# Transposing K and Q through a DRAM scratch by DMA instead of on TensorE, in an attention plus gMLP kernel

## The chip, the cores and the metric

The kernel runs on one core of one Trainium2 chip. The metric is device time in microseconds (us) of one execution; lower is better. Each comparison below was made with runs of the kernel before on the same chip in the same rounds, and "faster" or "slower" needs a difference of 2%. An interval in brackets is a 95% interval.

Engines are called by the profile's names: PE is TensorE, PEld its weight load, DVE VectorE, ACT ScalarE, POOL GpSimd, SP SyncE, which issues most DMAs here. "SPq" is SP's queue of DMA issues. "L326" is line 326 of the kernel's file. A line of the changed kernel has another number than the same line of the kernel before: the K and Q evacuation is L512 before and L523 after, the general matmul helper L326 and L328, the residual add L874 and L885.

## The reference, cut to what matters

```python
# q, k, v: (4 batches, 8 heads, 768, 64); blocks of 32; x: (4, 768, 512)
scores = (q @ k.transpose(0, 1, 3, 2)) / sqrt(64)
# kept: window |bi - bj| <= 1, first and last block row and column, 3 random key blocks per query block
attn = softmax(where(mask, scores, -1e9)) @ v
x = attn.transpose(0, 2, 1, 3).reshape(4, 768, 512)
h = gelu(x @ w_in); u, vv = h[..., :512], h[..., 512:]
vv = layernorm(vv) * g_ln
vv = einsum('ts,bsd->btd', w_sg, vv) + b_sg
return x + (u * vv) @ w_out
```

The scores need K and Q with the head dimension on the partitions, and they arrive with tokens on the partitions. So both have to be transposed, for each batch.

## The kernel before

A small list scheduler inside the kernel (`Plan`) is given every operation with a modelled duration, simulates the engines, and so fixes the order of instructions on each engine. On the chip every engine works through its list in that order and waits by semaphores. If something lands later than the model thought, whatever stands behind it on that engine waits too. The model of a DMA is one shared pipe:

```python
if o.dsem is not None:                     # a DMA
    b = max(free[e] + 0.9, dmafree)
    dmafree = b + o.bytes                  # nbytes / 390e3 us, or the op's own bw
    o.fin = dmafree + 1.1
```

An argument `aft=` orders operations in this plan only; it makes no semaphore. One use of it matters: the exponentials of a batch are planned after the last U gelu of the batch before, to save ACT table loads.

The parts that the change and the argument touch (cuts marked):

```python
def loads(b):                              # batches 1 to 3: POOL queue, f32 -> bf16 on the way
    ...
    for nm, t_, src in (("v", vn, v), ("k", kn, k), ("q", qn, q)):
        o = op("POOL", f"ld{nm}{b}", ..., w=[(nm + "n", n) for n in range(4)],
               nbytes=1572864, bw=265e3, aft=aft)

def transposes(b):
    for pp in range(4):
        for nm, n_ in (("k", kn), ("q", qn)):
            u = Unit("M")                  # one of two PSUM slots, shared with the MLP
            ...                            # 12 PE transposes into the slot
            op("PE", f"TR{nm}{b}.{pp}", tr, ...)
            # DVE empties the slot for K, ACT for Q, into KT / QT
            op("ACT" if nm == "q" else "DVE", f"e{nm}{b}.{pp}", ev, ...)
    op("DVE", f"eq{b}.d", ...)             # QT columns 768:800 <- 0:32
    op("DVE", f"ek{b}.g", kg, r=KT...)     # KG <- the first and last key block of KT
# kgather: the random key blocks, KR <- KT, copied by DVE (L596) and POOL (L600)
# weights2: w_sg and w_out loaded, planned after batch 1's loads of v, k and q
for b in range(4):
    ... attention of batch b; after its second tile loads(b + 1), vprep(b + 1) ...
    transposes(b + 1); vread(b + 1)
    if b == 0: weights2(hold["kq"], hold["kq"])
    ... MLP of batch b: V, U, spatial gate S (with w_sg), O (with w_out), residual add ...
```

I call the stretch from one batch's last exponential to the next batch's first one a handover. The MLP's V and U parts of the batch before, and most of the transposes, run in it.

The softmax here doesn't subtract the row's maximum and nothing guards it: scores larger than these inputs give would overflow.

Of the kernel before, what the change touches and what calls it, by code (L numbers as in the profile page):

```python
# [7 lines left out]
BF16 = mybir.dt.bfloat16  # L8
# [4 lines left out]
B, H, S, D = 4, 8, 768, 64  # L13
P, T = 128, 6
DM, DFF = 512, 1024
NB = 24
EPS = 1e-6
NRING = 16
NKR = 8
ORDERS = ((0, 1, 2, 3, 4, 5), (5, 0, 1, 2, 3, 4))  # L20
SPSET = (3, 6, 9, 12, 15, 18, 21)
# [18 lines left out]
class Plan:  # L40
# [10 lines left out]
    def op(self, eng, name, fn, r=(), w=(), dur=0.1, lat=0.0, prio=0, mode=None, alloc=None, use=None, dsem=None, nbytes=0, pre=(), nd=1, aft=(), bw=390e3):  # L51
        o = Op()
        o.eng, o.name, o.fn, o.dur, o.lat, o.prio, o.mode = eng, name, fn, dur, lat, prio, mode
        o.alloc, o.unit, o.dsem, o.bytes = alloc, use, dsem, nbytes / bw
        o.nd = nd
        o.start = o.fin = None
        o.idx = len(self.ops)
        deps = {}
        for k in r:
            x = self.lastw.get(k)  # L60
            if x is not None:
                deps[x.idx] = x
        for k in w:
            x = self.lastw.get(k)
            if x is not None:
                deps[x.idx] = x
            for x in self.readers.get(k, ()):
                deps[x.idx] = x
        if use is not None:
            use.readers.append(o)  # L70
        if dsem is not None:
            x = self.dlast.get(dsem)
            if x is not None:
                deps[x.idx] = x
            self.dlast[dsem] = o
        for k in w:
            self.lastw[k] = o
            self.readers[k] = []
        for k in r:
            self.readers.setdefault(k, []).append(o)  # L80
        o.deps = list(deps.values())
        aft = {x.idx: x for x in aft}
        for k in pre:
            for x in self.readers.get(k, ()):
                aft[x.idx] = x
        o.after = [x for x in aft.values() if x.idx not in deps]
        self.ops.append(o)
        return o
# [164 lines left out]
def bass_bigbird_attn__then__gmlp_full_block_kernel(  # L253
# [6 lines left out]
    op = pl.op  # L260

    def sb(name, shape, dt):
        return ctx.enter_context(nc.sbuf_tensor(name, shape, dt))
# [16 lines left out]
    qn = sb("qn", [P, H, T, D], BF16)  # L280
    kn = sb("kn", [P, H, T, D], BF16)
    vn = sb("vn", [P, H, T, D], BF16)
    vj = sb("vj", [P, T, H, 65], BF16)
    QT = sb("QT", [P, 4, 800], BF16)
    KT = sb("KT", [P, 4, 800], BF16)
    KG = sb("KG", [P, 4, P], BF16)
# [3 lines left out]
    VG = sb("VG", [P, 4, 130], BF16)  # L290
    VR = sb("VR", [P, NRING, H, 65], BF16)
    PW = [sb(f"PW{i}", [P, 1024], BF16) for i in range(4)]
    PR = [sb(f"PR{i}", [P, 1024], BF16) for i in range(3)]
    PG = [sb(f"PG{i}", [P, 512], BF16) for i in range(3)]
    rden = [sb(f"rden{i}", [P, 2, 4, 1], F32) for i in range(2)]
    lnst = sb("lnst", [P, 4, 6], F32)
    lnmv = sb("lnmv", [P, T, 2], F32)
# [14 lines left out]
    Mps = ctx.enter_context(nc.psum_tensor("Mps", [P, 1024], F32))  # L312
    Mbf = Mps.bitcast(BF16)
    scr = [nc.dram_tensor(f"scr{i}", (800, 520), BF16, kind="Internal").ap() for i in range(2)]
    pl.pool("S", 2)
    pl.pool("O", 1)
    pl.pool("M", 2)
# [47 lines left out]
    def c_bias1(vx):  # L365
# [8 lines left out]
       r=["VGz"] + [("VG", n) for n in range(4)], w=[("scz", 0)], dur=0.6, prio=-60, dsem="z0", nbytes=33000)  # L374

    op("SP", "sbi", lambda e: e.dma_start(sbi[:, :], sampled_blocks.bitcast(I32)), w=["sbi"], dur=0.6, prio=-300,
       dsem="c0", nbytes=600)
# [18 lines left out]
    def ixr(x):  # L396
# [7 lines left out]
       r=["effr", "ident"], w=["ixp"], dur=0.1, prio=-170, alloc=u_ix)  # L404
# [86 lines left out]

    def transposes(b):
        pr = 1000 * b - 350 if b else -70
        for pp in range(4):
            for nm, n_ in (("k", kn), ("q", qn)):
                u = Unit("M")
                TT = KT if nm == "k" else QT

                def tr(pe, pp=pp, n_=n_, u=u):
                    ins = None  # L500
                    for j in range(T):
                        c = u.slot * 1024 + j * P
                        for hp in range(2):
                            ins = pe.transpose(Mbf[64 * hp:64 * hp + 64, c:c + P], n_[:, 2 * pp + hp, j, :], ident[:, :])  # L504
                    return ins
                tk = [(nm.upper() + "T", pp)]
                op("PE", f"TR{nm}{b}.{pp}", tr, r=[(nm + "n", pp), "ident"], w=[("trp", nm, b, pp)], dur=0.36, prio=pr + pp, mode="64c", alloc=u, pre=tk)

                def ev(x, pp=pp, nm=nm, u=u, TT=TT):
                    o_ = TT[:, pp, 0:S].rearrange("p (t j) -> p t j", j=T)  # L510
                    i_ = Mbf[:, u.slot * 1024:u.slot * 1024 + S].rearrange("p (j t) -> p t j", t=P)
                    return x.activation(o_, i_, ACT.Copy) if nm == "q" else x.tensor_copy(o_, i_)  # L512
                op("ACT" if nm == "q" else "DVE", f"e{nm}{b}.{pp}", ev, r=[("trp", nm, b, pp)], w=tk, dur=0.86, prio=pr + pp, use=u)
        op("DVE", f"eq{b}.d", lambda x: x.tensor_copy(QT[:, :, 768:800], QT[:, :, 0:32]), r=[("QT", p_) for p_ in range(4)], w=[("QT", 4)], dur=0.15, prio=pr + 4)

        def kg(x):
            ins = None
            for hp in range(2):
                for i, c0 in enumerate((0, 736)):
                    ins = x.tensor_copy(KG[64 * hp:64 * hp + 64, :, 64 * hp + 32 * i:64 * hp + 32 * i + 32], KT[64 * hp:64 * hp + 64, :, c0:c0 + 32])  # L520
            return ins
        op("DVE", f"ek{b}.g", kg, r=[("KT", p_) for p_ in range(4)], w=["KG"], dur=0.5, prio=pr + 4)
# [30 lines left out]
    rgof, krof = {}, {}  # L553
    cnt = {"PW": 0, "PR": 0, "PG": 0, "gt": 0, "rd": 0, "KR": 0, "VR": 0}

    def ring(nm, n):
        x = cnt[nm] % n
        cnt[nm] += 1
        return x
# [4 lines left out]
    def vgather(n):  # L564
# [3 lines left out]
        if b == 0:  # L568
            pr = -20 + tau
        rg = n % NRING  # L570
        rgof[b, i] = rg
# [57 lines left out]
    def attention(b, tau, pos):  # L629
        bp = b % 2  # L630
        pr = 1000 * b + 100 * pos
# [5 lines left out]
        krs = [krof[b, i0 + ib] for ib in range(nbk)]  # L637
        qk = [("QT", t) for t in range(5)]
        kt = [("KT", t) for t in range(4)]
        pw, pg_, pr_ = ring("PW", 4), ring("PG", 3), ring("PR", 3)  # L640
        ga = hold.get("g", []) if b else []

        uW = Unit("S")
# [1 line left out]
        def qkw(pe):  # L645
            ins = None
            for pp in range(4):
                for g_ in range(ng):
                    for hp in range(2):
# [3 lines left out]
                        ins = mm(pe, Sps[:, c:c + 64], KT[r0:r0 + 64, pp, kc:kc + P],  # L653
                                 QT[r0:r0 + 64, pp, 32 + P * tau + 64 * g_:96 + P * tau + 64 * g_], True)
            return ins
        op("PE", f"qkW{b}.{tau}", qkw, r=qk + kt, w=[("sW", b, tau)],
           dur=0.015 * 8 * ng + 0.1, prio=pr, mode="64x128", alloc=uW, pre=[("PW", pw, 0), ("PW", pw, 1)])
# [15 lines left out]
        def qkg(pe):  # L673
            ins = None
            for pp in range(4):
                c = uG.slot * 1024 + pp * P
                ins = mm(pe, Sps[:, c:c + P], KG[:, pp, :], QT[:, pp, 32 + P * tau:160 + P * tau], True)
            return ins
        op("PE", f"qkG{b}.{tau}", qkg, r=qk + ["KG"], w=[("sG", b, tau)], dur=0.22, prio=pr + 1, mode="128", alloc=uG, pre=[("PG", pg_)])
        op("ACT", f"exG{b}.{tau}", aft=ga, fn=lambda a: a.activation(PG[pg_][:, :], Sps[:, uG.slot * 1024:uG.slot * 1024 + 512], ACT.Exp, scale=SCALE),  # L680
           r=[("sG", b, tau)], w=[("PG", pg_)], dur=0.6, prio=pr + 1, mode="exp", use=uG)

        uR = Unit("S")

        def qkr(pe):
            ins = None
            for pp in range(4):
                for ib in range(nbk):
                    for hp in range(2):
                        r0 = 64 * hp  # L690
                        c = sbank(uR, hp) + (pp * nbk + ib) * 32
                        qc = 32 * (i0 + ib)
                        ins = mm(pe, Sps[:, c:c + 32], KR[r0:r0 + 64, pp, krs[ib], :], QT[r0:r0 + 64, pp, qc:qc + 32], True)
            return ins
        op("PE", f"qkR{b}.{tau}", qkr, r=qk + [("KR", rg, j) for rg in krs for j in range(3)], w=[("sR", b, tau)],
           dur=0.013 * 8 * nbk + 0.1, prio=pr + 2, mode="64x128", alloc=uR, pre=[("PR", pr_)])
# [8 lines left out]
        if last:  # L705
            for c3 in range(3):
# [3 lines left out]
                def qkq(pe, c3=c3, uQ=uQ):  # L710
# [12 lines left out]
                   r=[("sQ", b, c3)], w=[("PW", pw3, 0), ("PW", pw3, 1)], dur=1.02, prio=pr + 3 + c3, mode="exp", use=uQ)  # L723
# [16 lines left out]
        def pvw(pe):  # L740
# [9 lines left out]
           w=[("Oa", b, tau)], dur=0.014 * 8 * ng + 0.05, prio=pr + 51, mode="64")  # L750

        def pvr(pe):
# [8 lines left out]
           dur=0.009 * 8 * nbk + 0.05, prio=pr + 52, mode="32")  # L761
        ow = [("Oa", b, tau), ("Ob", b, tau)]
        for c3, pw3 in enumerate(pq):
            def pvq(pe, c3=c3, pw3=pw3):
# [8 lines left out]
               w=[("Oq", b, c3)], dur=0.45, prio=pr + 53, mode="64")  # L773
# [3 lines left out]
           r=ow, w=[("rd", rd)], dur=0.13, prio=pr - 500, use=uO)  # L777
# [84 lines left out]
    def mlp_o(b, tau):  # L862
# [21 lines left out]

    loads(0)  # L885
    transposes(0)
    vprep(0)
    vread(0)
    op("POOL", "w_in", lambda g: g.dma_start(w_in[:, :, :], moe_w_in.rearrange("(a p) f -> p a f", p=P)), w=["w_in"], dur=1.2,
       prio=WP, dsem="w0", aft=[hold["sc"]], nbytes=2.1e6)  # L890
    ng = used = 0
    for b in range(B):
        for pos, tau in enumerate(ORDERS[b > 0]):
            while ng < len(gseq) and ng < used + NRING and gseq[ng][0] == b:
                vgather(ng)
                ng += 1
            if pos == 2 and b + 1 < B:
                loads(b + 1)
                vprep(b + 1)
            while ng < len(gseq) and ng < used + NRING and (gseq[ng][0] == b or pos > 2):  # L900
                vgather(ng)
# [5 lines left out]
        if b + 1 < B:  # L907
            transposes(b + 1)
            vread(b + 1)
            while ng < len(gseq) and ng < used + NRING:  # L910
                vgather(ng)
# [46 lines left out]
```

## Time and profile before

The recorded time before is 282.72 us (2 runs, 282.61 to 282.83). The prediction was made from a trace whose own execution took 316.53 us, with a span of 314.7 us. These are lines of that first page: the span, and the chain of work that ended last, by engine.

```profile
span 314.7 us, 8868 instructions
...
PE 58%; DVE 14%; issue 11%; ACT 9%; POOL 3%; another core or an unknown queue 2%; DVEq 1%; POOLq 0%; ACTq 0%
```

PE is the engine that most of the chain runs through, but 11% of the chain is "issue", time in which the engine waited for nothing that the profile shows. The table of busy time by stretches (columns: stretch; for each engine busy us and instructions; PE clock granted; DMA share; GB/s) gave the handovers of this trace (the first one is shown) and a dense stretch for comparison:

```profile
80.80:97.00 16.20, 7.94 (x145) 6.20 (x142) 6.99 (x27) 4.44 (x7) 8.88 (x12) 0.82 1.18 232
...
248.00:280.00 32.00, 29.87 (x736) 21.97 (x735) 20.73 (x60) 20.98 (x32) 7.49 (x18) 1.00 0.17 49
```

PE was busy about half of this handover stretch and nearly all of the dense one. That is the slack the change aims at.

For comparing with the kernel after I use a later trace of the same kernel from the 282 us chip (run b_third). Its page says:

```profile
span 282.4 us, 8868 instructions
PE 220.7 (78%) x3717; PEld 162.8 (58%) x3717; DVE 163.5 (58%) x468; ACT 149.1 (53%) x222; POOL 103.8 (37%) x204
DMA packets 34411, 41.29 MB, mean 146 GB/s; under 512 B 6548, under 2 KB 27700, under 8 KB 34372
PE 61%; DVE 16%; ACT 10%; DMA 5%; issue 3%; SPq 2%; POOL 1%; DVEq 0%; POOLq 0%; ACTq 0%
```

Here is its handover to batch 1 in the chain of work that ended last (columns: start us, us, what):

```profile
80.28 0.80 PE Mps L504 x11
81.10 0.82 ACT QT L512
...
88.88 0.87 PE Sps L326 x12
...
93.26 0.49 ACT uT L841
...
95.06 0.84 ACT PW L668 x2
```

Twelve transposes on PE (L504), an evacuation on ACT (L512), twelve more, and so on; then the last MLP matmuls, the last U gelu (L841) and the first exponential of batch 1 (L668) at 95.06 us. This alternation is what the change removes.

### The profile page before, as it was taken

The numbers are of one execution on the slowest core, as the hardware profiler recorded it, in microseconds if no ns is written. First come the engines' busy times: TensorE is split into PE (matmuls) and PEld (weight loads), VectorE is DVE, ScalarE is ACT, GpSimd is POOL, SyncE is SP. The second block draws the span as 40 slices with busy tenths as digits, with TensorE's granted clock in tenths as the row PEclk, the third lists the DMA queues.
The fourth block names the chain that finished last, engine by engine and source line by source line (L and its number), as shares of the span: only waits on it lengthen the run. The fifth ranks groups of instructions, "written<-read, shape, count | busy, mean of one in ns | idle before, by whom it ended". The sixth has DMA issues, their size and how long they took to land.

```text
span 314.7 us, 8868 instructions
## 1 busy us (share of the span) xinstructions
PE 234.8 (75%) x3717; PEld 171.5 (55%) x3717; DVE 163.7 (52%) x468; ACT 149.1 (47%) x222; POOL 104.8 (33%) x204
## 2 busy tenths in 40 slices
PE   1543047597737479787699999787799997999994
PEld 1432036485626357565355868565567675767642
DVE  6525013236533165425498657354477665758683
ACT  2587024356334752636212587455425874755200
POOL 1131777112183851542441222653403124102100
PEclk9999999969795758779799999899599999999999
DMA  6957863980999929331799102442711014111022
GB/s 205 374 164 288 230 162 78 173 133 40 195 275 242 308 33 214 86 92 38 206 210 261 64 6 50 133 122 60 211 68 32 4 27 120 37 69 35 0 100 100
DMA packets 34411, 41.29 MB, mean 131 GB/s; under 512 B 6548, under 2 KB 27700, under 8 KB 34372
## 3 DMA queue, kind: packets, MB, share of 16 engines
q0 software_dynamic: 14112, 17.40, 27.9%
q1 hardware_dynamic: 20260, 23.33, 24.0%
q8 instruction: 29, 0.48, 0.6%
q14 instruction: 10, 0.08, 0.1%
HBM read 39.45 MB, written 9.55 MB: 156 GB/s over the span
## 4 chain that ended last, share of the span: by engine, by line
PE 58%; DVE 14%; issue 11%; ACT 9%; POOL 3%; another core or an unknown queue 2%; DVEq 1%; POOLq 0%; ACTq 0%
PE Mps L326 28%; PE Ops L326 12%; PE Sps L326 9%; PE Mps L795 5%; PE Mps L504 4%; DVE gt L856 3%; ACT PR L700 2%; DVE xg L859 2%; DVE KT L512 2%; ACT QT L512 2%; POOL VR L579 1%; PE Mps L620 1%; DVE x_tok L780 1%; DVE x_tok L874 1%
## 5 line engine op out<-in xcount | busy, mean ns | idle before, releaser
L579 POOL DMA_INDIRECT VR<-scr,IDX x60 | 56.2, 937 | 56.7 <-PE Ops L326 29.7
L596 DVE COPY KR<-KT 128x128 bf16 x176 | 27.4, 230 | 38.7 <-PE Ops L326 20.8
L326 PE MATMUL Mps<-w_sgT,vh 128*128 128x384 bf16 x192 | 38.0, 345 | 2.7 <-DVE KT L512 1.8
L700 ACT ACTIVATE PR<-Sps 96x1024 bf16<-96x1024 f32 x20 | 20.4, 1020 | 32.9 <-PE Ops L326 21.6
L600 POOL COPY KR<-KT 128x128 bf16 x88 | 22.5, 296 | 39.1 <-PE Sps L326 27.1
L326 PE MATMUL Mps<-w_out,xg 128*128 128x512 f32 x96 | 28.6, 429 | 2.8 <-DVE xg L859 1.6
L326 PE MATMUL Mps<-xg,w_in 128*128 128x384 f32 x128 | 28.3, 375 | 2.5 <-ACT QT L512 2.0
L856 DVE SCALAR_TENSOR_TENSOR gt<-Mps,gcol,bsg 128x384 f32<-128x384 f32 x32 | 19.8, 618 | 17.8 <-PE Mps L326 15.6
L326 PE MATMUL Mps<-w_in,xg 128*128 128x512 f32 x96 | 27.6, 434 | 1.5 <-ACT xg L798 0.7
L326 PE MATMUL Sps<-QT,KR 64*128 64x32 bf16 x704 | 13.6, 178 | 19.2 <-POOL KR L600 9.7
L798 ACT ACTIVATE xg<-Mps 128x512 fp32r<-128x512 f32 x24 | 14.3, 596 | 28.3 <-PE Mps L795 21.0
L326 PEld LDWEIGHTS Mps<-xg,w_in 128*128 128x128 f32 x128 | 23.3, 205 | 6.9 <-ACT QT L512 2.3
L326 PEld LDWEIGHTS Mps<-w_sgT,vh 128*128 128x128 bf16 x192 | 17.6, 101 | 16.9 <-DVE KT L512 2.2
L814 ACT ACTIVATE vg<-Mps 128x512 f32<-128x512 f32 x24 | 14.0, 598 | 26.8 <-PE Mps L326 25.2
L326 PE MATMUL Sps<-QT,KT 64*128 64x64 bf16 x544 | 16.9, 209 | 12.7 <-issue 3.8
L821 POOL TENSOR_TENSOR lnt<-lnmv,lnc 128x2 f32<-128x2 f32 x12 | 3.0, 248 | 69.7 <-DVE lnmv L817 69.7
L512 DVE COPY KT<-Mps 128x768 bf16<-128x768 bf16 x16 | 15.1, 954 | 20.3 <-PE Mps L504 17.2
L326 PE MATMUL Ops<-VA,PW 128*64 128x65 bf16 x384 | 21.7, 206 | 3.9 <-issue 3.7
L326 PEld LDWEIGHTS Sps<-QT,KR 64*128 64x128 bf16 x704 | 10.9, 96 | 23.3 <-POOL KR L600 9.8
L326 PEld LDWEIGHTS Mps<-w_in,xg 128*128 128x128 f32 x96 | 18.0, 204 | 8.6 <-DVE x_tok L874 2.0
L326 PEld LDWEIGHTS Mps<-w_out,xg 128*128 128x128 f32 x96 | 16.9, 193 | 9.6 <-DVE xg L859 2.5
L326 PEld LDWEIGHTS Sps<-QT,KT 64*128 64x128 bf16 x544 | 12.1, 105 | 17.9 <-issue 5.5
(91 smaller groups left out, 414.0 us busy)
## 6 DMA issues: line engine op xcount, KB each, us to landing
out_dram<-x_tok SPq DMA_DIRECT2D x20, 256.0 KB, 2.1
scr<-vj SPq DMA_DIRECT2D x4, 780.0 KB, 5.0
VR<-scr SPq DMA_DIRECT2D x84, 32.5 KB, 3.3
VS<-scr SPq DMA_DIRECT2D x4, 650.0 KB
vn<-in_v_dram POOLq DMA_DIRECT2D x3, 768.0 KB, 9.1
kn<-in_k_dram POOLq DMA_DIRECT2D x3, 768.0 KB
qn<-in_q_dram POOLq DMA_DIRECT2D x3, 768.0 KB, 13.9
VA<-scr SPq DMA_DIRECT2D x4, 520.0 KB
```

Of the source, the lines that this page charges most:

```text
L326: return pe.matmul(o, l, r, start=start, stop=True, skip_group_check=True)
L504: ins = pe.transpose(Mbf[64 * hp:64 * hp + 64, c:c + P], n_[:, 2 * pp + hp, j, :], ident[:, :])
L512: return x.activation(o_, i_, ACT.Copy) if nm == "q" else x.tensor_copy(o_, i_)
L579: return g.indirect_dma_start(out=VR[0:96, rg, :, :].rearrange("p h e -> p (h e)"), out_offset=None, in_=scr[bp][:, :], in_offset=bass.Ind ...
L596: ins = x.tensor_copy(KR[:, :, rg, 32 * j:32 * j + 32], KT[:, :, bass.ds(vals["DVE", j, i], 32)])
L600: op("POOL", f"kp{b}.{i}", lambda x, i=i, rg=rg: x.tensor_copy(KR[:, :, rg, 64:96], KT[:, :, bass.ds(vals["POOL", 2, i], 32)]), r=kk + [(" ...
L700: return a.activation(PR[pr_][0:96, :], Sps[0:96, uR.slot * 1024:uR.slot * 1024 + 1024], ACT.Exp, scale=SCALE)
L795: ins = pe.transpose(Mps[:, cc:cc + P], x_tok[bp][:, tau, kt * P:kt * P + P], ident_f[:, :])
L798: op("ACT", f"xE{b}.{tau}", lambda a: a.activation(xg[c][:, :, tc * P:tc * P + P], Mps[:, u.slot * 512:u.slot * 512 + 512].rearrange("p (a ...
L814: op("ACT", f"gV{b}.{tau}", lambda a: a.activation(vg[vr][:, :], Mps[:, u.slot * 512:u.slot * 512 + 512], ACT.Gelu_apprx_tanh), r=[("vp", ...
L856: op("DVE", f"g1{b}.{c}{dt}", lambda x: x.scalar_tensor_tensor(gt[gr][:, :], Mps[:, u.slot * 512:u.slot * 512 + 384], gcol[:, dt:dt + 1], ...
L859: op("DVE", f"g2{b}.{c}{dt}", lambda x: x.tensor_tensor(xg[2 + c][:, dt, :], gt[gr][:, :], uT[c][:, dt, :], ALU.mult), r=[("gt", gr), ("uT ...
```

## The change

The intent is to free PE, the shared PSUM slots, DVE and ACT of the transposes of batches 1 to 3. DVE permutes K and Q once to token rows of 512 contiguous values, SP writes them to DRAM, and a transposing DMA brings each back as KT or QT. The space for the permuted copy `kj` comes from two rings (16 to 14 and 3 to 2 buffers). The diff, with its headers and one line that repeats a ring's size left out:

```diff
-NRING = 16
+NRING = 14
+    kj = sb("kj", [P, T, H, D], BF16)
-    PG = [sb(f"PG{i}", [P, 512], BF16) for i in range(3)]
+    PG = [sb(f"PG{i}", [P, 512], BF16) for i in range(2)]
+    skq = {nm: nc.dram_tensor(f"scr_{nm}", (768, 512), BF16, kind="Internal").ap() for nm in "kq"}
     def transposes(b):
         pr = 1000 * b - 350 if b else -70
-        for pp in range(4):
+        if b:
+            for nm, n_, TT in (("k", kn, KT), ("q", qn, QT)):
+                op("DVE", f"p{nm}{b}", lambda x, n_=n_: x.tensor_copy(kj[:, :, :, :], n_[:, :, :, :].rearrange("p h j d -> p j h d")),
+                   r=[(nm + "n", n) for n in range(4)], w=["kj"], dur=0.9, prio=pr - 300)
+                op("SP", f"w{nm}{b}", lambda e, nm=nm: e.dma_start(skq[nm].rearrange("(p j) c -> p (j c)", j=T), kj[:, :, :, :].rearrange("p j h d -> p (j h d)")),
+                   r=["kj"], w=[("skq", nm)], dur=0.6, prio=pr - 300, dsem=f"w{nm}", nbytes=786432)
+            for nm, TT in (("k", KT), ("q", QT)):
+                op("SP", f"T{nm}{b}", lambda e, nm=nm, TT=TT: e.dma_start_transpose(TT[:, :, 0:S], skq[nm]),
+                   r=[("skq", nm)], w=[(nm.upper() + "T", p_) for p_ in range(4)], dur=0.6, prio=pr, dsem="xbar", nbytes=786432)
+        for pp in range(4 if b == 0 else 0):
             for nm, n_ in (("k", kn), ("q", qn)):
```

There is one `kj` for K and Q, both reads share the semaphore `xbar`, so K is read before Q, and writes and reads all go through the in-order SP queue.

More of the change, by code (lines that the diff above doesn't have):

```diff
@@ L639, in attention @@
         kt = [("KT", t) for t in range(4)]
-        pw, pg_, pr_ = ring("PW", 4), ring("PG", 3), ring("PR", 3)
+        pw, pg_, pr_ = ring("PW", 4), ring("PG", 2), ring("PR", 3)
         ga = hold.get("g", []) if b else []
```

## The prediction

> **What bounds the kernel now.** One core, 282.7 us timed; the profiled execution spans 314.7 us, so I scale by 0.90. PE is busy 75% of the span and holds 58% of the chain that ended last (busy section, chain). Away from handovers PE is nearly full (table of busy time by stretches: 17.5 of 18 us in 227 to 245, 29.9 of 32 in 248 to 280). It is loose where one batch hands over to the next: 7.9 of 16.2 us in 80.8 to 97.0, 9.4 of 14.4 in 142.8 to 157.2, 9.5 of 13.3 in 213.7 to 227.0. There, groups of twelve transposes alternate with their evacuations through two PSUM slots that the MLP shares.
>
> **Removed** (same table, restricted to the transpose and evacuation lines): per batch 96 PE transposes, 5.5, 4.0 and 5.3 us of PE; four DVE evacuations of 0.96 us and four ACT ones of 0.81 us. Total 14.8 us PE, 11.3 us DVE, 9.6 us ACT.
>
> **Added**: per batch two DVE permutes (the same-shaped V permute takes 0.94 us, so 5.7 us in all), two DRAM writes of 786 KB (the like V write lands in 5.0 us) and two transposing reads, K then Q, in series on the SP queue. No such read is in this trace. The Trainium skill, "DMA: Bandwidth & Descriptors", section "Latency and other measured facts", gives 261 GB/s for a transpose with a non-contiguous middle dimension; my estimate is 786 KB / 261 GB/s + 2 us = 5 us each. "VectorE: DVE Perf Modes", section "The three transpose paths", gives 1309 ns for one 128x128 tile; 24 unoverlapped tiles would be 31 us. I expect 5 to 9 us each. DMA bytes rise by 9.4 MB on 41 MB. The V-gather ring shrinks from 16 to 14 and PG from 3 to 2: I allow 1 to 2 us.
>
> **Critical path.** The writes can go early. The reads must wait for the last QK matmul and key gather of the batch before. But the next batch's exponentials wait for the last U gelu, and before that stand 13 us of V and U matmuls, so 10 to 18 us of reads are about hidden. I take 4 to 5 us each for batches 2 and 3 and 4 to 6 for batch 1, where the DMA engines are saturated (share 1.18 in 80.8 to 97.0). Sum about 14 us profiled, 12 timed, less 1 to 2 for the rings and about 2 for late data: the instruction orders are fixed by a model that assumes 390 GB/s for the read; if it lands later, DVE and POOL stand at the key gathers, with layer norm work behind them.
>
> **Prediction: 274 us, 8 in 10 between 262 and 290.** Chances: faster by over 2% 0.60, within 2% 0.22, slower by over 2% 0.18.
>
> **What would show each step.** Right: PE transposes of K and Q fall from 384 to 96; PE busy falls by about 15 us; the loose handovers shrink from 13 to 16 us to about 9; the reads land in 5 to 9 us; KG and KR copies do not wait on DMA. Wrong: DVE or POOL waits of several us for the KT read, each batch; PE waiting for QT; SP occupied for long by the transposes, with V gathers or output stores late.
>
> **What would make it wrong.** Reads of 15 us and more: each handover waits for them, up to 300 us. Or batch 2's loads, released earlier because K and Q come free at the permute, crowd batch 1's reads. Or the list scheduler reorders MLP and attention work so that PE gains nothing.

## The result

The recorded result is 305.62 us after (304.95 to 306.30) against 282.72 us before, a ratio of 1.081 [1.0706, 1.0914]: slower by 8%. Ratios here and below are the mean time of one kernel's fast runs over that of the other's of the same rounds, so they are not quite the ratio of the medians quoted beside them. The prediction had the wrong sign and 305.62 lies outside its range.

The trace compared here is from the repeat on the 282 us chip (run a_third, 303.36 us against 282.13, ratio 1.0743), because the kernel before was traced on that same chip in that same job. The lines of its page that answer to those of b_third:

```profile
span 300.8 us, 8290 instructions
PE 219.2 (73%) x3429; PEld 160.8 (53%) x3429; DVE 156.7 (52%) x462; ACT 140.1 (47%) x210; POOL 105.7 (35%) x204
DMA packets 53897, 50.69 MB, mean 169 GB/s; under 512 B 25268, under 2 KB 46420, under 8 KB 53860
PE 50%; DMA 21%; DVE 11%; SPq 6%; ACT 6%; issue 3%; DVEq 1%; POOL 1%; ACTq 0%
```

The work did go: 288 PE instructions, 6.8 us of DVE and 9.0 us of ACT. PE's busy time fell by only 1.5 us, although the transposes had cost 14.4 us in three stretches of b_third (6.6, 4.0 and 3.8 us); the mean granted clock was 0.946 there and 0.881 here, and two of the four large groups of MLP matmuls became longer (w_in with xg: 425 ns each before, 486 ns after; w_out with xg: 423 and 446), while the other two became a little shorter. The chain moved from PE to DMA, from 5% of the span to 21%, with 6% more on SP's queue. About 18,700 more packets are under 512 bytes: 3,120 for each of the six reads, so 252 bytes each if a read's 786,432 bytes are divided by that.

Where did the 18.4 us of span come from? I cut both traces at ACT's markers: the first exponential of each batch, and the first gelu table load after each batch's exponentials (us):

| stretch | before (b_third) | after (a_third) | difference |
|---|---|---|---|
| start to first exponential of batch 1 | 95.1 | 128.8 | +33.8 |
| attention of batch 1 | 40.2 | 27.1 | -13.1 |
| handover to batch 2 | 28.9 | 26.9 | -2.0 |
| attention of batch 2 | 34.0 | 30.8 | -3.2 |
| handover to batch 3 | 20.0 | 22.3 | +2.3 |
| attention of batch 3 and tail | 64.3 | 64.8 | +0.5 |

Almost all of the loss sits in the handover to batch 1, which came 33.8 us later; 13.1 us of it came back in the row of batch 1's attention. PE's work on the tile Mps (MLP and transposes) in that row fell from 16.5 to 3.5 us: about 4.0 us of this are the removed transposes of batch 2, the rest is MLP work of batch 0 that had already been done during the wait.

The marker hides something at the other two handovers. In b_third the transposes of batches 2 and 3 ran before the gelu table load, so they are counted under "attention" (none lies in the two later handover rows). Counted from the last exponential, as a handover was defined above, the handover to batch 2 took 37.4 us before and 26.9 us after, and that to batch 3 27.0 and 25.7 us. How much of the first difference is the transposes, and how much MLP work done earlier, the two traces do not separate. The rows "attention of batch 2" and "handover to batch 3" together gained 0.9 us, where 3.8 us of PE transposes went.

The same place in the chain of work that ended last, after:

```profile
81.87 30.95 DMA KT<-scr_k
112.85 0.04 DVE KG L531
...
128.35 0.11 DVE QT L525
...
128.84 0.84 ACT PW L679 x2
```

One read of K takes 30.95 us of the chain. The waits in 78 to 114 us say who stood still for it (columns: engine, line, what it waited for; total us, times, longest). The lines are from the tables of DVE, POOL and PE.

```profile
DVE x_tok L624 <- DMA x_tok<-in_moe_w_sg_dram: 10.9, 1, 10.9
DVE KG L531 <- DMA KT<-scr_k: 7.1, 1, 7.1
POOL KR L611 <- DMA KT<-scr_k: 17.7, 1, 17.7
PE Mps L631 <- DVE x_tok L624: 13.1, 1, 13.1
```

DVE stood first 10.9 us for the weight w_sg, then 7.1 us for K; PE waited 13.1 us on the first of these. And Q was behind K. SP's timeline (start us, duration us, what) shows it:

```profile
81.87 21.88 SPq L503 DMA_TRANSPOSE KT<-scr_k  x1
103.81 0.56 SPq L500 DMA_DIRECT2D scr_q<-kj  x1
...
114.52 3.79 SPq L503 DMA_TRANSPOSE QT<-scr_q  x1
```

The transposing read held SP's queue for 21.88 us, and the write of Q could only be issued at 103.81, so the read of Q at 114.52. Q landed 5.9 us later, at 120.4. DVE was by then busy with MLP work that had also been held up, so the copy of Q's first columns (L525, the last thing the first score matmuls need) came at 128.35, in DVE's fixed order. The Trainium skill, "DMA: Bandwidth & Descriptors", section "Issuing engines are not separate DMA queues", says that all queues end on the same 16 DMA engines and interleave, and that the sequencer's time to initiate a DMA is usually small beside the DMA. The trace agrees with the first half: during K's read the queue of POOL's DMAs (software_dynamic in the profile) took 82% of the 16 engines' time and that of SP's (hardware_dynamic) 38%. It differs on the second for a transposing read: 21.9 of 31.0 us.

Busy time by stretches gives the DMA load, first for the kernel before in its handover, then after (columns as above):

```profile
71.00:95.00 24.00, 16.68 (x196) 13.63 (x196) 10.04 (x32) 10.75 (x15) 13.13 (x20) 0.64 1.17 244
```

```profile
82.00:113.00 31.00, 10.93 (x72) 6.61 (x72) 9.78 (x19) 1.23 (x1) 10.84 (x12) 0.73 1.20 243
```

The DMA engines were just as full before (share 1.17, 244 GB/s), but then K and Q of batch 1 were already on the chip, and PE did not depend on those queues. In the changed kernel K's transposing read joins this traffic. What is in it, by the list of DMA issues of 60 to 130 us (KB each, median us to landing):

```profile
kn<-in_k_dram POOLq DMA_DIRECT2D x2, 768.0 KB, 15.8
w_out<-in_moe_w_out_dram POOLq DMA_DIRECT2D x1, 1024.0 KB, 26.2
x_tok<-in_moe_w_sg_dram POOLq DMA_DIRECT2D x1, 960.0 KB, 23.4
...
KT<-scr_k SPq DMA_TRANSPOSE x1, 31.0
```

Two kinds of traffic compete: the weights, which landed at 92.8 to 97.6 us, and the loads of later batches; the last of these, V of batch 3, landed at 112.4 us, just before K's read (112.8). POOL's timeline shows why they meet K's read now. First before, then after:

```profile
76.39 0.88 POOL L487 DMA_DIRECT2D kn<-in_k_dram  x1 [6.45 <-PE Mps L504]
77.26 0.88 POOL L607 DMA_DIRECT2D x_tok<-in_moe_w_sg_dram  x1
...
103.40 0.94 POOL L487 DMA_DIRECT2D qn<-in_q_dram  x1
```

```profile
68.54 0.90 POOL L489 DMA_DIRECT2D kn<-in_k_dram  x1
69.42 0.90 POOL L618 DMA_DIRECT2D x_tok<-in_moe_w_sg_dram  x1
...
93.25 0.99 POOL L489 DMA_DIRECT2D qn<-in_q_dram  x1
```

Before, batch 2's load of K waited 6.45 us for the PE transposes to let go of the buffer `kn`, and the weights stood behind it. Now the permute has freed the buffer, so K and the weights go out 8 us earlier; and Q of batch 2 and V of batch 3 (93.25 and 94.20) go out 10 us earlier, into the middle of K's read.

At handovers 2 and 3 the reads take 8.3 and 9.8 us (K) and 5.9 and 6.9 us (Q), which is near what was predicted. Little was gained even so. The waits of 207 to 228 us, in the handover to batch 3:

```profile
PE Mps L328 <- DVE x_tok L885: 5.4, 1, 5.4
DVE KG L531 <- DMA KT<-scr_k: 4.8, 1, 4.8
```

and DVE's timeline there (start us, us, instruction, in brackets the idle time before it and its releaser):

```profile
212.30 0.69 DVE L885 TENSOR_TENSOR x_tok<-Mps,x_tok 128x512 f32<-128x512 f32 x1
217.81 0.86 DVE L531 COPY KG<-KT 64x128 bf16<-64x128 bf16 x4 [4.81 <-DMA KT<-scr_k]
...
219.87 0.68 DVE L885 TENSOR_TENSOR x_tok<-Mps,x_tok 128x512 f32<-128x512 f32 x1
```

The plan expected K's read (issued at 207.95) after 0.9 + 786432 / 390,000 + 1.1 us and SP's 0.6, 4.6 us in all; it landed at 217.81, after 9.8. DVE's list is fixed, so the copy KG waits 4.81 us, the residual add L885 behind it still holds its PSUM slot, and PE waits 5.4 us for that slot. The PE transposes removed for batch 3 had cost 3.8 us.

### The profile page after: what moved, and what is told of

Its sections match the earlier page's. It is cut to its first block, busy times and chain, and to the rows that moved or that the text cites. A ratio compares the mean times of both kernels' runs of the same rounds, so it can differ in the third digit from the quotient of the medians.

```text
span 303.1 us, 8290 instructions
## 1 busy us (share of the span) xinstructions
PE 220.3 (73%) x3429; PEld 161.3 (53%) x3429; DVE 156.6 (52%) x462; ACT 139.9 (46%) x210; POOL 106.5 (35%) x204
## 4 chain that ended last, share of the span: by engine, by line
PE 49%; DMA 21%; DVE 11%; ACT 6%; SPq 6%; issue 4%; POOL 1%; DVEq 0%; POOLq 0%; ACTq 0%
PE Mps L328 27%; DMA KT<-scr_k 13%; PE Ops L328 9%; PE Sps L328 8%; DMA scr<-vj 4%; PE Mps L806 3%; SPq L552 3%; DVE gt L867 2%; ACT PW L679 2%; DMA QT<-scr_q 2%; DMA VR<-scr 2%; DVE xg L870 2%; PE Mps L515 2%; SPq L585 1%; ACT vg L825 1%
## 5 line engine op out<-in xcount | busy, mean ns | idle before, releaser
L590 POOL DMA_INDIRECT VR<-scr,IDX x60 | 57.7, 961 | 38.1 <-PE Ops L328 13.7
L679 ACT ACTIVATE PW<-Sps,b_odd 128x512 bf16<-128x512 f32 (+1 forms) x24 | 15.6, 651 | 55.7 <-PE Sps L328 54.8
L328 PE MATMUL Mps<-w_sgT,vh 128*128 128x384 bf16 x192 | 36.7, 339 | 1.0 <-DVE w_sgT L634 0.7
L328 PE MATMUL Mps<-w_in,xg 128*128 128x512 f32 x96 | 32.0, 486 | 6.4 <-DVE x_tok L885 4.4
L607 DVE COPY KR<-KT 128x128 bf16 x176 | 25.2, 215 | 17.4 <-PE Sps L328 16.9
L328 PEld LDWEIGHTS Mps<-w_in,xg 128*128 128x128 f32 x96 | 21.0, 234 | 13.9 <-DVE x_tok L885 5.1
L867 DVE SCALAR_TENSOR_TENSOR gt<-Mps,gcol,bsg 128x384 f32<-128x384 f32 x32 | 19.8, 618 | 16.1 <-PE Mps L328 15.3
L328 PE MATMUL Mps<-xg,w_in 128*128 128x384 f32 x128 | 27.0, 364 | 0.2 <-ACT vg L825 0.2
L328 PE MATMUL Sps<-QT,KT 64*128 64x64 bf16 x544 | 16.5, 206 | 12.6 <-DVE QT L525 6.0
L825 ACT ACTIVATE vg<-Mps 128x512 f32<-128x512 f32 x24 | 14.0, 597 | 23.8 <-PE Mps L328 22.6
L787 DVE RECIPROCAL rden<-Ops 128x8 f32<-128x8 f32 x24 | 4.9, 205 | 34.6 <-PE Ops L328 34.6
L885 DVE TENSOR_TENSOR x_tok<-Mps,x_tok 128x512 f32<-128x512 f32 x24 | 16.5, 689 | 11.8 <-PE Mps L328 11.6
L806 PE MATMUL Mps<-ident_f,x_tok 128*128 128x128 f32 x96 | 17.8, 317 | 5.6 <-DVE x_tok L791 2.1
```

The lines of the kernel that those rows point to most:

```text
L328: return pe.matmul(o, l, r, start=start, stop=True, skip_group_check=True)
L590: return g.indirect_dma_start(out=VR[0:96, rg, :, :].rearrange("p h e -> p (h e)"), out_offset=None, in_=scr[bp][:, :], in_offset=bass.Ind ...
L607: ins = x.tensor_copy(KR[:, :, rg, 32 * j:32 * j + 32], KT[:, :, bass.ds(vals["DVE", j, i], 32)])
L679: return a.activation(o, i_, ACT.Exp, bias=bias[:, 0:1], scale=SCALE)
L806: ins = pe.transpose(Mps[:, cc:cc + P], x_tok[bp][:, tau, kt * P:kt * P + P], ident_f[:, :])
L825: op("ACT", f"gV{b}.{tau}", lambda a: a.activation(vg[vr][:, :], Mps[:, u.slot * 512:u.slot * 512 + 512], ACT.Gelu_apprx_tanh), r=[("vp", ...
```

## The experiments

Theories before the experiments, with the letters of the quoted expectations. A: batch 1's reads are slow because batch 2's loads (let in early) and the weights crowd them, and Q's write waits behind K's read on SP. B: the transposing read is slow in itself. C: the smaller rings cost the time. Two were added later. D: the key gathers stand too early in DVE's and POOL's lists. E, its rival: handovers 2 and 3 are limited by something else. "Fast chip" and "slow chip" there are the 282 us and the 321 us chip. All runs gave correct results; e_quiet's extra reads are of data that nobody uses.

| run | chip | us (median) | before, same job | ratio [95%] |
|---|---|---|---|---|
| b_again (before) | 321 | 320.35 | 321.84 | 0.9981 [0.9877, 1.0086] |
| e_mem | 321 | 315.04 | 321.84 | 0.984 [0.9742, 0.9938] |
| e_b23 | 321 | 305.24 | 321.84 | 0.9461 [0.9365, 0.9557] |
| e_hold | 321 | 310.96 | 321.84 | 0.9685 [0.9611, 0.9759] |
| a_again (after) | 321 | 323.61 | 320.68 | 1.012 [1.0034, 1.0207] |
| e_b1 | 321 | 344.81 | 320.68 | 1.0801 [1.0713, 1.0889] |
| e_quiet | 321 | 323.09, one run | 320.68 | none |
| b_third (before) | 282 | 283.16 | 282.13 | 1.0027 [0.9923, 1.0132] |
| a_third (after) | 282 | 303.36 | 282.13 | 1.0743 [1.0636, 1.0849] |
| e_b23h | 282 | 281.90 | 282.13 | none given; 278.43 to 284.86 |
| e_late | 321 | 320.54 | 321.06 | 1.0024 [0.9945, 1.0104] |
| e_hold2 (= e_hold) | 321 | 311.12 | 321.06 | 0.9709 [0.9651, 0.9768] |
| e_hold_late | 321 | 307.29 | 321.06 | 0.9566 [0.9472, 0.966] |
| e_b23h_late | 321 | 306.34 | 321.06 | 0.9578 [0.9507, 0.9649] |
| e_hold3 (= e_hold) | 282 | 291.30 | 282.30 | 1.0329 [1.0268, 1.039] |
| e_hold_late3 (= e_hold_late) | 282 | 285.30 | 282.30 | 1.0105 [1.0046, 1.0165] |
| e_hold_late_we | 282 | 282.63 | 282.30 | 1.004 [0.9975, 1.0105] |
| e_b23h_lat3 | 282 | 279.54 | 282.30 | 0.9886 [0.9798, 0.9974] |

By the rule of 2%, e_b23, e_hold, e_hold2, e_hold_late and e_b23h_late are faster, all on the 321 us chip; e_b1, a_third and e_hold3 are slower; e_mem, a_again and e_b23h_lat3 are unclear; those left with a ratio are the same. The medians include runs labelled slow (one each in e_b23 and e_b23h_lat3, two in e_b23h); the ratios do not.

Every edit below is against the kernel after.

### b_again: the kernel before once more

No edit.

> The kernel before, unchanged, for a second trace, because its first profiled execution spanned 314.7 us while its timed runs took 282.7. All theories: 282 to 284 us timed. If the profile spans about 283 us, the first trace was an odd execution and this one is to be compared with; if it spans about 315 us again, the profiler itself costs this kernel 30 us.

Measured: 320.35 us, like the 321.84 us of its own job and 13% above the recorded 282.72. The waits put down to "issue" on PE, in the table of waits of the whole span, first b_again and then b_third:

```profile
PE Ops L326 <- issue: 12.5, 23, 1.2
PE Sps L326 <- issue: 4.4, 5, 2.8
```

```profile
PE Ops L326 <- issue: 2.0, 2, 1.3
PE Sps L326 <- issue: 1.0, 1, 1.0
```

On the 321 us chip PE pauses for 20.9 us in all (three smaller entries, of 2.2, 1.4 and 0.4 us, are not shown) with no wait that the trace shows, mostly within dense streams of small matmuls of attn @ v (Ops); on the 282 us chip for 3.0 us. The first trace, from which I predicted, has 19.8 us of it. What causes the pauses was not found. The kernel before loses 38 us by this condition and the kernel after 20 us, which is why their ratio is 1.012 on one chip and 1.074 on the other.

### e_mem: all transposes on PE, the small rings and kj kept

```diff
-        if b:
+        if b in ():
-        for pp in range(4 if b == 0 else 0):
+        for pp in range(0 if b in () else 4):
```

> All batches transposed by PE as before, but with the rings of 14 and 2 and the unused permute buffer of the changed kernel. Theories A and B: 281 to 286 us. Theory C (the smaller rings cost the time): 295 us and more.

Measured: 0.984, not slower than before. The rings do not explain the loss, and the 1 to 2 us that the prediction allowed for them are not seen on this chip. (It was not run on the 282 us chip; e_b23h_lat3, which has the small rings too, was no slower than before there.) Why it is a little quicker was not traced; a changed plan may be all of it.

### e_b23 and e_b1: the change for batches 2 and 3 alone, and for batch 1 alone

```diff
-        if b:
+        if b in (2, 3):            # e_b1: if b in (1,):
-        for pp in range(4 if b == 0 else 0):
+        for pp in range(0 if b in (2, 3) else 4):     # e_b1: (1,)
```

> Batches 2 and 3 transposed by DMA, batch 1 by PE as before. Theory A (the loss is batch 1's handover, where the transposing reads share the DMA engines with the weight loads and the next batches' loads): at or under the kernel before, 270 to 281 us. Theory B (the transposing read is slow in itself, every handover pays): about two thirds of the loss stays, 293 to 300 us. Theory C (the smaller rings): 295 us and more.

> Only batch 1 transposed by DMA, batches 2 and 3 by PE. With all batches by PE (and the smaller rings) the ratio to the kernel before was 0.984, with batches 2 and 3 by DMA 0.946. Theory A (the loss sits in batch 1's handover): the ratio is 1.03 or more, and the K read of batch 1 lands 20 us or more after its issue. Theory B (every handover pays the same): not above 1.0.

Measured on 321 us chips: e_b23 0.9461, e_b1 1.0801. Against e_mem (315.04 us, in e_b1's case from another job and chip) the batches 2 and 3 bring 9.8 us and batch 1 costs 29.8 us, where the whole change costs 8.6 us. The parts do not add. In e_b1 batch 2's handover row is 41.3 us (25.0 in a_again), and its trace shows batch 2's PE transposes inside it: eight groups that alternate with their evacuations from 178.3 to 192.9 us. Counted from the last exponential, e_mem's own handover to batch 2 takes 36.3 us. The sign is clear: batch 1 does the harm, and batches 2 and 3 gain on this chip. In e_b1 K's read for batch 1 took 31.3 us and held SP for 22.2 us, the same event as above, although no other batch was read by transposing DMA.

### e_hold: each batch's loads planned after the Q read of the batch before

```diff
-                op("SP", f"T{nm}{b}", lambda e, ...
+                hold[b + 1] = [op("SP", f"T{nm}{b}", lambda e, ...       # loads(b + 1) is planned after it
```

> The changed kernel, with the loads of K, Q and V of batch b+1 planned after the transposing read of Q of batch b, so that the loads of batches 2 and 3 leave batch 1's handover; the weight loads stay there. Theory A: most of the loss goes, 272 to 288 us, and batch 1's K read lands within 20 us of its issue instead of 31. Theory B: little changes, 298 to 306 us.

> The second and third batch's loads kept out of batch 1's handover, as in the first job, once more because the conditions differ between chips. Theory A: on a chip where the kernel before takes 283 us, ratio 1.01 to 1.04 (the changed kernel has 1.074); on a slow chip 0.97 as measured before.

> Once more the changed kernel with the later batches' loads held back, for a chip where the kernel before takes 283 us. Theory A: ratio 1.01 to 1.04 there (the changed kernel has 1.074); 0.97 again on a slow chip.

Measured: 0.9685 and 0.9709 on 321 us chips (the change itself: 1.012) and 1.0329 on the 282 us chip (1.0743), about 4 hundredths better in each. SP's timeline of e_hold3:

```profile
80.92 3.71 SPq L503 DMA_TRANSPOSE KT<-scr_k  x1
84.67 0.57 SPq L500 DMA_DIRECT2D scr_q<-kj  x1
...
98.37 11.96 SPq L503 DMA_TRANSPOSE QT<-scr_q  x1
```

K's read of batch 1 now holds SP for 3.71 us and lands in 9.7 us, not 31.0; Q's write goes out at 84.67. So what had made it slow is what the edit moved: batch 2's loads, and with them the weights. The expectation that the weight loads stay was wrong: no longer behind batch 2's V and K, they landed at 79 to 84 us, not at 93 to 98. The share of all DMA engines during K's read was no lower (1.18 in e_hold3, 1.20 in a_third); what fell is the share that POOL's own queue took, from 82% to 44%. But Q's read still takes 18.6 us, with POOL's queue at 79%. POOL's timeline shows two of three loads just ahead of it (the third, of Q, at 96.66):

```profile
94.81 0.95 POOL L489 DMA_DIRECT2D vn<-in_v_dram  x1
95.76 0.93 POOL L489 DMA_DIRECT2D kn<-in_k_dram  x1
```

The edit holds the loads back in the plan, not on the chip. POOL's list reached them at 94.81 us, before SP's list reached Q's read at 98.37, since Q's write had landed later than planned. A version that holds them by a semaphore was not run. Batch 1's first exponential comes at 117.7 us: 11.1 us earlier than in a_third, still 22.6 us later than before the change.

### e_quiet: the transposing read by itself

Three more transposing reads of K's scratch, each followed by a plain read of the same bytes, were put behind the attention of the last batch.

```diff
+    for i in range(3):
+        op("SP", f"TX{i}", lambda e: e.dma_start_transpose(KT[:, :, 0:S], skq["k"]), ..., dsem="xq")
+        op("SP", f"PX{i}", lambda e: e.dma_start(kj[...], skq["k"]...), r=[("skq", "k"), ("KT", 0)], ..., dsem="xq")
```

> The changed kernel with three more transposing reads of K's scratch and three plain reads of the same 786 KB, alternating, each waiting for the one before, put behind the last QK matmul of batch 3 where the DMA engines are nearly idle; their data is not used. Theory A (crowding makes the reads late): the transposing read lands in 5 to 7 us, the plain one in 4 to 5. Theory B (the transposing read is slow in itself): 10 us and more with nothing beside it. The time of the whole kernel says nothing here.

Measured: the three transposing reads landed in 5.2, 6.2 and 7.0 us, the plain reads in 4.4 to 5.2 us. So the transposing read is not slow in itself, and theory B falls. The figure I had used (261 GB/s with a non-contiguous middle dimension, the Trainium skill, "DMA: Bandwidth & Descriptors", "Latency and other measured facts"), from which I estimated 5 us, lies just under what a quiet queue gave. The other figure, 1309 ns for one 128x128 tile (the Trainium skill, "VectorE: DVE Perf Modes", "The three transpose paths"), times 24 tiles would be 31 us; 24 tiles landed in 6.2 us when it was quiet, so that figure does not add up tile by tile here. That the crowded read also took 31 us is chance.

### e_late: key gathers planned after Q's read has landed

```diff
-        op("DVE", f"ek{b}.g", kg, r=...
+        op("DVE", f"ek{b}.g", kg, aft=hold.get(("T", b), []), r=...
-            op("DVE", f"kr{b}.{i}", kc, r=...
+            op("DVE", f"kr{b}.{i}", kc, aft=hold.get(("T", b), []), r=...      # and the same for POOL's kp
```

(`hold["T", b]` is set to the read of Q.)

> The changed kernel, with the KG copy and the key gathers on DVE and POOL planned after the Q read of the same batch instead of after the K read, so that in the fixed order of DVE and POOL the MLP's work stands in front of them. Theory D (at handovers 2 and 3 the freed PE time is lost because DVE stands about 5 us at the KG copy while the residual adds behind it hold PSUM slots that PE needs): 5 to 9 us faster than the changed kernel, so ratio 1.045 to 1.055 where the changed kernel has 1.074 (fast chip) or 0.985 to 0.995 where it has 1.012 (slow chip); PE's wait on the residual add after the KT read goes. Rival E (handovers 2 and 3 are limited by something else, SP or the next exponentials): unchanged within 1%.

Measured: 1.0024 on a 321 us chip, 0.010 better than a_again, some 3 us and less than expected; the two intervals overlap, so this is not clear of the noise. DVE's wait for K in the whole span of a_again (first) and of a_third shows why there was less to win on that chip:

```profile
DVE KG L531 <- DMA KT<-scr_k: 7.1, 1, 7.1
```

```profile
DVE KG L531 <- DMA KT<-scr_k: 14.3, 3, 7.1
```

In a_again the copy waits once, at batch 1; on the 282 us chip three times.

### e_hold_late: both edits

> Both repairs together, all three batches by DMA. Theories A and D: they add, so 5 to 9 us under the run with the loads held back alone, ratio 0.98 to 1.01 on a fast chip, 0.94 to 0.96 on a slow one. Rival E: no gain over the loads held back alone.

> Loads held back and gathers after the Q read, once more for a fast chip. Theories A and D: 3 to 8 us under the run with the loads held back alone, ratio 0.985 to 1.02 on a fast chip; 0.957 again on a slow one. Rival E: equal to it on a fast chip.

Measured: 0.9566 on the 321 us chip, and on the 282 us chip 1.0105 against 1.0329 for e_hold3 in the same job, 6.0 us less. The handover to batch 3 fell from 18.3 to 14.7 us and that to batch 1 came 6.7 us earlier. KG's waits for K are gone (12.9 us in three waits in e_hold3), and in the handover to batch 3 the copies now stand behind the residual adds:

```profile
202.41 0.69 DVE L885 TENSOR_TENSOR x_tok<-Mps,x_tok 128x512 f32<-128x512 f32 x1 [1.28 <-PE Mps L328]
...
205.85 0.57 DVE L531 COPY KG<-KT 64x128 bf16<-64x128 bf16 x4
```

At batches 2 and 3 this is a direct test of the fixed order: the read of K was hardly quicker there (10.0 us for batch 2 against 10.4, 6.5 us for batch 3 against 6.8), and in the handover to batch 3 PE's wait of 2.2 us for the residual add went with KG's wait. At batch 1 it is not: there Q's read fell from 18.6 to 13.3 us, where the new lists sent two of batch 2's loads ahead of it and not three, and of the 8.8 us between the two traces that handover makes 6.7. On the 321 us chip the same edit gave 3.8 us (e_hold_late against e_hold2, one job).

### e_hold_late_we: the weights early as well

```diff
-            weights2(hold["kq"], hold["kq"])
+            weights2([hold["sc0"]], [hold["sc0"]])      # planned after batch 0's V write
```

> As the one before, and the weight loads (w_sg and w_out, 3.4 MB of DRAM reads) moved ahead to the first attention phase, so that batch 1's handover holds neither weights nor later loads. Theory A: the first exponential of batch 1 comes 10 us or more earlier than with the loads held back alone, batch 1's Q read lands within 8 us, ratio 0.95 to 0.99 on a fast chip, 0.92 to 0.95 on a slow one. If the weights were not part of the crowding: no change, or slower, because they now crowd the first batch's value reads.

Measured: 1.004 [0.9975, 1.0105], a miss (0.95 to 0.99 expected). Batch 1's first exponential comes at 103.1 us, against 111.0 in e_hold_late3, and Q's read of batch 1 takes 11.4 us instead of 13.3. This is not the weights alone: in e_hold3 three of batch 2's loads went out ahead of Q's read, in e_hold_late3 two, and here one, and Q's read took 18.6, 13.3 and 11.4 us. Only 2.7 us of those 7.9 reach the end, because the attention of batch 3 grew to 39.7 us (31.5); the two intervals overlap. In that stretch PE has 3.4 us more of work on Mps and waits 3.7 us for DVE's layer norm (no such wait in e_hold_late3); why the work came to stand there was not found.

### e_b23h, e_b23h_late and e_b23h_lat3: batch 1 on PE, batches 2 and 3 by DMA

All three keep PE transposes for batch 1 and the held loads. e_b23h_late adds the late gathers; e_b23h_lat3 instead tells the planner that the reads land 3 us later:

```diff
-                o.fin = dmafree + 1.1
+                o.fin = dmafree + 1.1 + o.lat      # the reads get lat=3
```

> Batches 2 and 3 by DMA, batch 1 by PE, and the loads of batch 3 planned after batch 2's transposing read of Q. If crowding is what makes the reads late (theory A), this is at least as fast as batches 2 and 3 by DMA alone: ratio to the kernel before 0.92 to 0.95 in conditions like those of the first two jobs. Theory B: 0.95 to 0.98, nothing gained by moving loads.

> Batch 1 by PE, batches 2 and 3 by DMA, batch 3's loads held back, key gathers after the Q read. Theories A and D: the best of all, 3 to 6 us under the same without the late gathers, which had the time of the kernel before on a fast chip: ratio 0.975 to 0.99 there, 0.92 to 0.94 on a slow chip. Rival E: ratio 1.0 on a fast chip.

> Batch 1 by PE, batches 2 and 3 by DMA, loads of batch 3 held back, and the planner told that a transposing read lands 3 us later than it assumed, so that KG, key gathers and the QT copy all move back in the fixed order. Theory D: DVE's waits on KT and QT fall under 3 us together; ratio 0.97 to 0.99 on a fast chip, 0.93 to 0.95 on a slow one. Rival E: 1.0 on a fast chip.

Measured: e_b23h 281.90 us on the 282 us chip, in two pairs around 279 and 284.5, so a small gain is neither shown nor excluded. e_b23h_late 0.9578 on a 321 us chip, a miss (0.92 to 0.94 expected, "the best of all"): e_b23, without held loads and late gathers, had 0.9461 there, and the intervals overlap, so with batch 1 on PE the two repairs showed no gain. e_b23h_lat3 0.9886 [0.9798, 0.9974] on the 282 us chip: the best ratio there, 1% quicker than the kernel before, which the rule of 2% calls unclear. In it the reads took 10.9 and 10.0 us (K), 9.1 and 7.7 us (Q); the added 3 us of the plan were still too few for K, and DVE's waits for KT and QT came to 5.4 us, not under 3.

### a_again, b_third, a_third: the pair again on two chips

No edits.

> The changed kernel, unchanged, on one chip with the kernel before, because the kernel before takes 282.7 us in the runs first given and about 321 us in the job of the first experiments. If the first comparison holds within one job, the ratio is 1.08 and this takes about 345 us where the kernel before takes 320. If the two sides of the first comparison stood in different conditions of the chip, the ratio falls towards 1.0 or under it: the changed kernel's own traced run of 305 us beside 282.7 would then be a run in unlike conditions.

> The kernel before, unchanged, once more on another chip if the job gets one: it took 282.7 us in the runs first given and 318 to 324 us in the two jobs since. If it takes about 283 here, its trace is the one to hold against the changed kernel's first trace (305 us), and I expect hardly any of the PE pauses for which the profile shows no wait (22 and 21 us at matmuls in the slow traces, under 7 us then).

> The changed kernel, unchanged, in the same job: 305 us where the kernel before takes 283, 323 where it takes 320.

Measured: 1.012 on a 321 us chip, and 1.0743 [1.0636, 1.0849] on a 282 us chip, which agrees with the recorded 1.081. Its control b_third was 1.0027. On every kernel run on both kinds of chip (after, e_hold, e_hold_late) the ratio on the 321 us chip is lower by 0.054 to 0.064. So differences between kernels are only taken within one kind of chip.

## Why the prediction was wrong, point by point

- **"10 to 18 us of reads are about hidden", with a gain of "4 to 6" us for batch 1: this step failed.** The two reads with Q's write between them ran from 81.87 to 120.4 us. K's read took 31.0 us; "The writes can go early" failed for Q, whose write could not be issued until K's read let go of SP (103.8 us); and the first exponential of batch 1 came 33.8 us later. In the next row 13.1 us came back, about 4.0 of them batch 2's removed transposes: a loss of 21 to 25 us where a gain of 5 was written down. The prediction saw a DMA share of 1.18 in that very stretch and still charged the read its quiet price. That it named the danger ("batch 2's loads ... crowd batch 1's reads") makes it a wrong weight: e_hold3 shows that this crowd, the weights that queued behind it included, is worth some 12 us of 21 (1.0743 to 1.0329, times 282).
- **"4 to 5 us each for batches 2 and 3": seen on the 321 us chip, not on the 282 us chip.** On the kind of chip that the first trace came from, e_b23 is 9.8 us under e_mem, as was forecast for two batches; counted from the last exponential, its handovers to batches 2 and 3 are 4.9 and 6.7 us shorter. On the 282 us chip the two rows that held batch 3's transposes gained 0.9 us in a_third, and with batch 1 left on PE no run there was clearly faster than before. The mechanism that took gain at batch 3 was named ("DVE and POOL stand at the key gathers, with layer norm work behind them") but put at about 2 us in all. It measured 4.81 us of DVE and 5.4 us of PE in the handover to batch 3. Removing it by order shortened that handover by 3.6 us (e_hold_late3 against e_hold3); the 6.0 us of the whole run contain a quicker batch 1.
- **The size of the reads.** Right in the quiet tail and nearly right at handovers 2 and 3 of a_third (5.2 to 7.0 us quiet, 5.9 to 9.8 us there; "5 to 9" predicted), wrong by a factor of three to six for the one that mattered.
- **"Less 1 to 2 for the rings": not seen.** e_mem, on the 321 us chip, was not slower.
- **"PE busy falls by about 15 us": not seen.** It fell by 1.5 us, with a lower granted clock and slower MLP matmuls. Counting removed PE work as removed time was the weaker half of the argument anyhow.
- **The scaling by 0.90.** The trace and the quoted time came from two conditions of the chip, and some 20 us of the trace were pauses that the quicker condition does not have. The plan of handovers was read from the wrong trace; a scale factor cannot mend that.
- Right: PE instructions fell by 288 (three times 96), the bytes rose by 9.4 MB, K's scratch write landed in 4.7 us in the median (5.0 predicted; Q's in 7.4), and the sign that was to show the prediction wrong ("SP occupied for long by the transposes") is exactly what the trace shows.

What is shown: the handover of batch 1 is the loss; the edit that puts batch 2's loads later, which also lets the weights land earlier, gives back about half of it; in the handover to batch 3 the fixed order of the gathers held up PE. What is only argued: that this order is all that handovers 2 and 3 lacked on the 282 us chip, and how the crowd divides between the weights and the loads (e_hold_late_we changed both, moved the handover by 7.9 us, and its total is within error of e_hold_late3). What stays open: the pauses of PE on the 321 us chip, why the gain of batches 2 and 3 is seen there and not on the other, and the longer attention of batch 3 in e_hold_late_we. No version with all three batches read by transposing DMA beat the kernel before on the 282 us chip; on the 321 us chip e_hold and e_hold_late did.

## What to carry to other kernels

Moving work from a compute engine to DMA takes it off a queue you have profiled and puts it on one you may not have: charge the transfer the time that other transfers take in the very stretch where it will run (for the weights, 16.3 and 20.1 us in the first trace), not its quiet time, and ask what the buffers freed earlier will let in. Where instruction orders are fixed beforehand, what counts is not when the data lands but what stands behind the first instruction that waits for it; putting the consumers later in the list shortened one handover by 3.6 us with hardly any change to the transfer. And compare the profile's own execution time with the quoted times before reading anything from it.

## What the Trainium skill lacked or had wrong

- "DMA: Bandwidth & Descriptors" has a bandwidth for the transposing DMA and, outside a table about trn3, nothing on how long it holds the queue that issues it. Here it held SP for 3.2 to 4.1 us in the quiet tail (a plain read of the same bytes: 0.35 to 0.37 us) and for 21.9 us among POOL's loads. The same page's sentence that the time to initiate a DMA is usually small beside the DMA does not fit this kind.
- The same page gives no landing time for such a read among other DMAs. The same 786 KB took 5.2 to 7.0 us in a quiet queue, 5.9 to 9.8 us at handovers 2 and 3 of a_third (up to 14.5 us in other runs) and 31.0 us at batch 1. The share of busy DMA engines does not tell these apart: it was 1.20 for the 31.0 us, 1.18 for the 9.7 us of e_hold3, and 0.92 for a read alone.
- "Advanced Engine Details and Errata", section "X-Bar Transpose (TRN2)", calls transposing DMAs "as fast as regular DMAs". Alone, 5.2 to 7.0 us against 4.4 to 5.2 us for a plain read of the same bytes: close, but slower.
- No page that I read says how many packets a profile counts for the transposing read: here about 3,120 for 786 KB, some 250 bytes each.
- No page that I read mentions that one kernel can take 282 us on one chip and 321 us on another with all runs of each in agreement, nor the PE pauses without a visible wait that go with it (3.0 us against 20.9 us).
